# Spreading softmax reciprocals over the partitions: one transfer per tile over 128 partitions in place of halves of 64, with a new operation sequence

## The chip, the cores and the metric

One core of one Trainium2 chip runs the whole program. The time is device microseconds of that core, the median of several executions; most executions of one kernel here agree within 0.5%. Where a ratio is given, it is the mean time of one kernel's runs over the mean of the other's of the same rounds on the same chip, so it is not quite the ratio of the medians quoted beside it.

## The reference

Attention over 4 batches, 8 heads, 768 positions and 64 features, followed by a layer with a swish in the middle. Three heads (0, 2, 6) see every earlier key, the other five see 4 sink keys and a window of 64.

```python
scores = scale * np.matmul(q, k.transpose(0, 1, 3, 2))
scores = np.where(mask[None], scores, -1e9)
a = np.exp(scores - np.max(scores, axis=-1, keepdims=True))
a = a / (np.sum(a, axis=-1, keepdims=True) + 1e-09)      # the division that this case is about
x = np.matmul(a, v)  # -> [4 * 768, 8 * 64]
h = x @ w_in                                             # 512 -> 2048
out = (h / (1 + np.exp(-beta * h))) @ w_out              # 2048 -> 512
```

## The kernel before

The work is cut into 8 units of 384 positions (units 2b and 2b+1 are the halves of batch b). A unit's attention result lies in PSUM as four tiles of 128 partitions x 384 positions; a tile holds two heads, one on partitions 0 to 63 and one on 64 to 127. It must be multiplied by 1/sum, and 1/sum is one number per head and position, so it has to be copied to the 64 partitions of its head. From unit 2 on this is done with transfers: sums out of PSUM, gathered into a compact tile (`rec`), reciprocal, out to DRAM (`rd`), and back with every row read 64 times (`R`). That last step is "the spread".

```python
PAIRS/XT: x tile t holds the heads XT[t] = [(1, 0), (2, 3), (4, 5), (6, 7)][t]
ORDER = [[1, 0, 2, 3, 4, 5, 6, 7], [2, 6, 0, 3, 5, 7, 1, 4]]    # rows of rd, even and odd units

def sums_turn(x):                     # gather: 8 rows of 384 -> 96 partitions of 32
    for p, step, c, n in ([(0, 16, 0, 8)], [(96, 1, 3, 5), (0, 32, 0, 3)])[x.u]:
        sp.dma_start(out=x.rec[c * CR:(c + n) * CR, :],
                     in_=x.sc[p:p + (n - 1) * step + 1:step, :].rearrange("p (c n) -> p c n", n=32))

def spread_w(x):                      # reciprocals to DRAM
    sp.dma_start(out=x.rd.rearrange("h (c n) -> (h c) n", n=32), in_=x.rec)

def spread_r(x):                      # the spread: halves of 64 partitions
    for i in range(2):
        ...                           # which tiles one transfer can take
        for t in ts:
            sp.dma_start(out=x.R[i * D:(i + 1) * D, t, :],
                         in_=bass.AP(..., [[0, D], [(a[1] - a[0]) * NQ, len(a)], [1, NQ]]))

def norm(x, g):                       # tiles 0, 1 (g = 0) and 2, 3 (g = 1)
    dve.tensor_mul(x.xT[:, 2 * g:2 * g + 2, :], o[:, :, 0:NQ], x.R[:, 2 * g:2 * g + 2, :])

def mm1(x, fi):                       # first layer; needs all four tiles of xT
    for pi in range(NP):
        pe.matmul(h[:, 0:NQ], w_in_sb[...], x.xT[:, pi, :], start=(pi == 0), stop=(pi == NP - 1))
# ... everything else cut
```

Each engine is given its instructions in a fixed order. That order comes from a list, `SEQUENCE`, which was searched with estimated costs; so the list is part of the tuning, and the estimates for the spread (`dma=[4.1, 4.4]`) decide how much other work stands between the spread and its use. All stores, transposes and spreads, and all loads but four of k, are issued by SyncE, one after the other.

The softmax here doesn't subtract the row's maximum and nothing guards it: scores larger than these inputs give would overflow.

Of the kernel before, what the change touches and what calls it, by code (L numbers as in the profile page):

```python
# [20 lines left out]
NQ = 384  # L21
# [7 lines left out]
QUARTERS = [[[1, 0], [2, 3], [4, 5], [6, 7]], [[2], [6], [0], [3, 5, 7, 1, 4]]]  # L29
ROWS = [16, 1]  # L30

NE = [16, 24]
ORDER = [[1, 0, 2, 3, 4, 5, 6, 7], [2, 6, 0, 3, 5, 7, 1, 4]]
# [4 lines left out]
    474, 475, 0, 2, 468, 10, 8, 6, 4, 469, 473, 14, 466, 477, 463, 471, 12, 81, 1, 478, 77, 25, 3, 16, 26, 9,  # L38
    33, 11, 479, 20, 35, 34, 5, 27, 18, 36, 28, 7, 29, 42, 31, 30, 13, 53, 480, 32, 82, 15, 50, 41, 37, 51,
    464, 38, 54, 52, 44, 17, 45, 47, 39, 48, 85, 23, 46, 24, 79, 40, 49, 78, 56, 89, 21, 104, 55, 57, 490, 19,  # L40
    43, 58, 59, 22, 100, 60, 61, 101, 482, 62, 83, 476, 80, 91, 73, 63, 90, 485, 102, 74, 75, 484, 64, 103,
    76, 116, 465, 117, 65, 118, 66, 86, 67, 69, 119, 120, 491, 87, 68, 492, 122, 70, 71, 481, 123, 72, 483,
    121, 470, 125, 494, 520, 500, 84, 493, 126, 106, 524, 107, 105, 521, 93, 528, 525, 489, 532, 526, 486, 95,
    128, 127, 529, 112, 92, 88, 522, 97, 536, 530, 113, 495, 114, 537, 108, 115, 109, 124, 129, 538, 503, 540,
    501, 110, 541, 547, 111, 488, 542, 487, 548, 131, 134, 94, 132, 551, 505, 130, 135, 549, 137, 98, 138,
    139, 502, 555, 533, 133, 142, 140, 136, 504, 534, 559, 552, 141, 143, 510, 563, 96, 553, 556, 560, 144,
    99, 467, 561, 496, 155, 557, 499, 564, 145, 497, 157, 498, 156, 506, 515, 523, 146, 507, 570, 509, 527,
    565, 508, 571, 169, 147, 158, 531, 572, 161, 148, 149, 535, 511, 163, 150, 512, 151, 167, 153, 152, 574,
    513, 165, 514, 154, 578, 575, 159, 582, 173, 576, 579, 171, 586, 580, 583, 518, 218, 584, 517, 587, 516,
    588, 519, 592, 596, 593, 539, 597, 168, 543, 546, 170, 544, 550, 164, 598, 222, 188, 160, 554, 594, 189,  # L50
    162, 558, 166, 172, 184, 562, 185, 174, 186, 600, 187, 190, 193, 181, 191, 566, 196, 569, 192, 573, 175,
    194, 604, 220, 567, 198, 605, 219, 577, 601, 201, 221, 581, 199, 197, 585, 602, 225, 589, 200, 228, 608,
    590, 195, 606, 224, 203, 609, 612, 223, 204, 227, 610, 619, 202, 206, 613, 205, 623, 226, 620, 207, 614,
    176, 627, 621, 208, 177, 591, 628, 568, 631, 178, 624, 209, 629, 179, 210, 635, 625, 632, 545, 636, 633,
    229, 237, 637, 642, 239, 646, 238, 235, 650, 182, 643, 240, 647, 644, 595, 241, 211, 648, 654, 212, 242,
    472, 269, 599, 651, 249, 655, 652, 658, 236, 250, 656, 232, 603, 286, 252, 183, 607, 659, 254, 230, 660,
    213, 611, 257, 243, 251, 615, 255, 231, 180, 618, 622, 616, 273, 256, 626, 253, 244, 630, 245, 634, 247,
    246, 638, 258, 248, 641, 639, 645, 287, 233, 259, 617, 214, 260, 216, 215, 261, 649, 272, 653, 217, 271,
    280, 657, 234, 664, 276, 668, 288, 665, 661, 279, 669, 666, 275, 672, 662, 270, 676, 278, 670, 673, 262,
    680, 274, 677, 674, 684, 678, 277, 681, 691, 685, 682, 281, 695, 263, 686, 692, 699, 326, 283, 696, 693,  # L60
    703, 697, 700, 707, 704, 701, 714, 663, 705, 708, 718, 289, 715, 709, 722, 716, 290, 726, 264, 293, 667,
    719, 291, 671, 720, 675, 727, 329, 723, 730, 728, 315, 282, 724, 679, 731, 292, 328, 295, 732, 683, 284,
    298, 687, 296, 690, 294, 694, 319, 297, 300, 688, 698, 301, 285, 702, 303, 299, 265, 302, 304, 267, 327,
    689, 266, 305, 330, 268, 706, 306, 710, 307, 713, 711, 717, 370, 736, 317, 740, 721, 741, 321, 725, 737,
    318, 324, 729, 738, 322, 742, 733, 331, 316, 744, 325, 734, 748, 320, 745, 308, 752, 749, 746, 323, 756,
    750, 753, 763, 757, 754, 309, 767, 366, 758, 764, 771, 768, 765, 775, 769, 772, 779, 712, 773, 332, 786,
    780, 790, 776, 781, 334, 310, 777, 787, 739, 336, 788, 794, 335, 798, 791, 368, 377, 337, 795, 743, 369,
    339, 796, 747, 792, 338, 373, 802, 799, 346, 803, 800, 751, 349, 640, 804, 755, 333, 347, 350, 759, 367,
    762, 760, 341, 371, 766, 344, 340, 770, 374, 372, 342, 774, 345, 348, 351, 375, 778, 343, 354, 782, 376,
    352, 355, 313, 783, 353, 311, 378, 383, 356, 312, 785, 784, 357, 314, 789, 358, 793, 808, 812, 412, 816,  # L70
    813, 387, 817, 814, 797, 390, 386, 801, 388, 820, 818, 359, 392, 389, 821, 360, 805, 809, 416, 822, 395,
    824, 810, 391, 393, 828, 415, 806, 835, 829, 394, 839, 414, 836, 830, 397, 837, 361, 825, 843, 840, 826,
    847, 841, 844, 851, 845, 858, 396, 384, 811, 418, 815, 848, 379, 421, 398, 819, 849, 413, 859, 860, 852,
    862, 807, 853, 866, 863, 399, 870, 400, 419, 864, 867, 823, 871, 422, 874, 872, 364, 401, 417, 868, 875,
    362, 876, 420, 385, 402, 380, 363, 827, 735, 403, 365, 831, 404, 834, 832, 838, 423, 381, 842, 846, 429,
    880, 382, 833, 884, 881, 888, 885, 850, 886, 431, 882, 889, 854, 405, 432, 890, 857, 406, 861, 433, 426,
    865, 425, 855, 869, 424, 856, 430, 761, 873, 427, 434, 436, 892, 407, 877, 435, 896, 878, 893, 900, 897,
    894, 879, 907, 898, 901, 911, 908, 902, 915, 909, 912, 919, 916, 913, 923, 917, 920, 930, 924, 921, 934,
    925, 938, 935, 942, 931, 410, 932, 936, 408, 939, 883, 943, 409, 887, 411, 946, 891, 940, 443, 947, 952,
    446, 948, 895, 944, 444, 956, 953, 960, 954, 899, 445, 961, 447, 438, 962, 903, 439, 437, 906, 964, 441,  # L80
    440, 910, 904, 957, 448, 442, 905, 914, 428, 449, 918, 451, 922, 965, 452, 450, 926, 958, 453, 927, 966,
    929, 928, 454, 933, 455, 968, 972, 969, 979, 970, 937, 980, 983, 981, 941, 984, 945, 973, 985, 987, 974,
    456, 991, 988, 457, 995, 992, 989, 949, 993, 996, 955, 997, 1002, 950, 1006, 1003, 959, 1007, 1004, 458,
    1010, 1008, 1014, 1011, 1018, 1015, 1012, 963, 1016, 1019, 951, 967, 1020, 971, 975, 978, 976, 982, 977,
    986, 990, 994, 998, 1001, 999, 1005, 459, 461, 460, 1009, 462, 1013, 1017, 1021, 1024, 1022, 1028, 1025,
    1023, 1032, 1000, 1029, 1026, 1036, 1030, 1033, 1040, 1037, 1034, 1044, 1038, 1041, 1051, 1045, 1042,
    1055, 1046, 1052, 1059, 1056, 1053, 1063, 1057, 1060, 1067, 1064, 1061, 1073, 1065, 1068, 1076, 1027,
    1077, 1069, 1031, 1074, 1078, 1079, 1075, 1082, 1080, 1085, 1083, 1081, 1035, 1084, 1086, 1039, 1087,
    1043, 1047, 1050, 1048, 1054, 1049, 1058, 1062, 1066, 1070, 1088, 1071, 1089, 1072, 1092, 1090, 1091,
# [3 lines left out]
    "dggdaaadgddddaddaddagddaaagaaaggddggddaadaddddaggadaaddggddggaggadddadgaddaaadddaaadaadddddaadaaa"  # L93
# [95 lines left out]
def kernel(  # L189
# [557 lines left out]
    def sums_d(x):  # L747
# [4 lines left out]
        for g, heads in enumerate(QUARTERS[x.u]):  # L752
            ops = []
            for i, h in enumerate(heads):
                r = ROWS[x.u] * i
                if RETR[h]:
                    ops += [(one[:, 31 - r:63 - r], q0, n, e) for (kb, q0, n, e) in x.work[h]]
                else:
                    ops += [(one[:, 31 - r:63 - r], 0, NQ, x.work[h]), (one[:, 31 - r:63 - r], None, NE[x.u], x.edge[h])]
            assert ops[0][1:3] == (0, NQ)  # L760
            todo.append(ops)
# [17 lines left out]
    def sums_turn(x):  # L779

        x.rec = rp.tile([8 * CR, 32], F32, name="rec")
        for p, step, c, n in ([(0, 16, 0, 8)], [(96, 1, 3, 5), (0, 32, 0, 3)])[x.u]:
            sp.dma_start(out=x.rec[c * CR:(c + n) * CR, :],
                         in_=x.sc[p:p + (n - 1) * step + 1:step, :].rearrange("p (c n) -> p c n", n=32))
# [8 lines left out]
    def spread_r(x):  # L793
# [3 lines left out]
        for i in range(2):  # L797
            d = at[i][1] - at[i][0]
            ts = [slice(0, NP)] if all(at[i][t] == at[i][0] + t * d for t in range(NP)) else [slice(0, 3, 2), slice(1, 4, 2)]
            for t in ts:  # L800
                a = at[i][t]
# [160 lines left out]
    add = plan.add  # L962
# [278 lines left out]
```

## Time and profile before

| | before |
|---|---|
| median of 3 runs | 244.12 us (243.6 to 245.04) |
| span of the profiled run | 242.7 us |
| TensorE busy | 226.1 us, 93% |
| granted TensorE clock, mean | 0.993 |
| first issue of a spread to its last landing, six units | 6.4 to 8.6 us |

How to read the lines: PE is TensorE, PEld its weight loads, DVE VectorE, ACT ScalarE, POOL GpSimd, and SPq SyncE issuing transfers. `out<-in` names what is written and what is read: `wf`, `q2f`, `k2f` and `vf` are loads of q, k, v and the weights, `c` and `vb` their copies in 16 bits, `QK` the transposed queries and keys, `KP` a packed copy of keys, `sp` and `b` results in PSUM, `xT` the normalised tiles, `osb` an output block on its way to DRAM. The granted clock is the share of its full clock that TensorE was allowed. "The chain" starts at the last instruction and is followed back, at each step, to what released it. In the kernel before it consists of:

```profile
PE 50%; DMA 24%; SPq 12%; DVE 4%; POOL 4%; issue 2%; ACT 1%; ACTq 0%; POOLq 0%; DVEq 0%
```

Half of the chain is TensorE at work, and most of the rest lies in the first 145 us, where loads, and SyncE's issuing of them, are the last thing that something waited for. The grouped waits (who waited for whom: total, times, longest):

```profile
POOL c L112 <- DMA wf<-in_q_dram: 15.7, 4, 13.5
...
POOL KP L112 <- DMA QK<-c: 13.7, 3, 6.0
POOL vb L112 <- DMA wf<-in_v_dram: 13.6, 7, 5.7
...
ACT osb L112 <- DMA out_dram<-osb: 4.1, 2, 2.1
...
PE sp L112 <- DMA QK<-c: 1.8, 2, 1.0
...
PE b L112 <- DVE xT L112: 1.3, 2, 1.1
```

GpSimd waiting for loads costs nothing as long as TensorE does not wait for GpSimd, and it hardly does: the largest group of such waits, weight loads that wait for a weight's 16-bit copy, adds up to 2.1 us.

### The profile page before, as it was taken

The page shows a single profiled execution, that of the slowest core. Times are in us where ns is not written, and L with a number is a line of the kernel's source. Part 1 is how long each engine was busy: PE and PEld are TensorE (multiplying, and loading weights), DVE is VectorE, ACT ScalarE, POOL GpSimd, SP SyncE. Part 2 cuts the span into 40 slices and gives each one's busy share as a digit, 9 for nine tenths or more (in the row PEclk, how much of TensorE's full clock was granted, in tenths as well). Part 3 has the DMA queues.
Part 4 walks back from the last instruction along what each step waited for, and adds up shares of the span by engine and source line. Part 5 has one row for each costly group of instructions (what it writes and reads, how often), then busy time and mean ns, then how long its engine had stood idle before and what let it go on. Part 6 is the DMA issues. An engine that isn't in the chain of part 4 may idle for free.

```text
span 242.7 us, 6088 instructions
## 1 busy us (share of the span) xinstructions
PE 226.1 (93%) x2388; PEld 127.7 (53%) x2388; DVE 158.8 (65%) x359; ACT 137.9 (57%) x231; POOL 87.5 (36%) x201
## 2 busy tenths in 40 slices
PE   7795889899979989899999989999999999999994
PEld 6562456455544445446554545564465455455553
DVE  4895789864786759479575457787566847336620
ACT  3657686266859607562489548745674745208611
POOL 6204757595791937354717300624200000000000
PEclk9999799999999999999999999999999999999999
DMA  6999699999979997999999999999720110802012
GB/s 208 272 321 333 199 252 349 290 289 198 190 199 178 217 172 167 194 244 198 237 179 246 205 167 178 212 175 240 203 61 3 43 45 7 221 3 86 0 43 86
DMA packets 92108, 43.14 MB, mean 178 GB/s; under 512 B 75936, under 2 KB 84848, under 8 KB 92080
## 3 DMA queue, kind: packets, MB, share of 16 engines
q1 hardware_dynamic: 90992, 41.98, 75.8%
q10 hardware_dynamic: 1088, 0.79, 1.0%
q8 instruction: 18, 0.29, 0.5%
q14 instruction: 10, 0.08, 0.1%
HBM read 32.38 MB, written 6.37 MB: 160 GB/s over the span
## 4 chain that ended last, share of the span: by engine, by line
PE 50%; DMA 24%; SPq 12%; DVE 4%; POOL 4%; issue 2%; ACT 1%; ACTq 0%; POOLq 0%; DVEq 0%
PE b L112 46%; SPq L112 12%; DMA wf<-in_moe_w_in_dram 9%; PE sp L112 4%; DMA wf<-in_v_dram 3%; DMA R<-rd 3%; DMA vf<-in_v_dram 3%; DMA wf<-in_k_dram 2%; DMA k2f<-in_k_dram 2%; DVE gT L112 2%; DMA QK<-c 2%; POOL w_in L112 2%; POOL c L112 2%; ACT t L112 1%; DVE xT L112 1%
## 5 line engine op out<-in xcount | busy, mean ns | idle before, releaser
L112 ACT ACTIVATE t<-b,beta_h 128x384 f32<-128x384 f32 x128 | 72.4, 583 | 47.9 <-PE b L112 36.1
L112 DVE SCALAR_TENSOR_TENSOR gT<-t,b 128x384 bf16<-128x384 f32 x128 | 68.8, 551 | 40.4 <-ACT t L112 36.8
L112 PE MATMUL b<-xT,w_in 128*128 128x384 bf16 x512 | 92.8, 330 | 2.0 <-POOL w_in L112 1.3
L112 PE MATMUL b<-w_out,gT 128*128 128x512 bf16 (+1 forms) x400 | 91.7, 371 | 0.0
L112 PEld LDWEIGHTS <-w_in 128*128 128x128 bf16 x512 | 49.4, 99 | 39.6 <-issue 3.9
L112 PEld LDWEIGHTS <-gT 128*128 128x128 bf16 x400 | 37.0, 98 | 38.5 <-issue 2.2
L112 ACT ACTIVATE es<-sp 128x768 bf16<-128x768 f32 (+2 forms) x64 | 48.6, 806 | 12.7 <-PE sp L112 12.5
L112 POOL CAST c<-wf 128x256 bf16<-128x256 f32 x60 | 22.5, 422 | 26.3 <-DMA wf<-in_q_dram 15.7
L112 PE MATMUL sp<-QK 64*64 64x64 bf16 (+6 forms) x402 | 18.8, 233 | 4.8 <-DMA QK<-c 1.8
L112 ACT ACTIVATE osb<-b 128x512 f32<-128x512 f32 (+1 forms) x13 | 7.4, 566 | 23.0 <-PE b L112 18.9
L112 PEld LDWEIGHTS <-QK 64*64 64x64 bf16 (+1 forms) x402 | 10.1, 105 | 15.5 <-issue 12.1
L112 POOL CAST vb<-wf 128x512 bf16<-128x512 f32 x18 | 12.1, 689 | 15.5 <-DMA wf<-in_v_dram 13.6
L112 DVE TENSOR_TENSOR es<-es,mask_c 128x256 bf16<-128x256 bf16 (+2 forms) x32 | 14.4, 457 | 4.1 <-ACT es L112 3.9
L112 POOL COPY KP<-QK 128x64 bf16<-128x64 bf16 (+5 forms) x38 | 10.6, 328 | 16.3 <-DMA QK<-c 13.7
L112 DVE TENSOR_TENSOR xT<-sp,R 128x768 bf16<-128x768 f32 (+3 forms) x18 | 11.6, 684 | 7.3 <-PE sp L112 5.8
L112 POOL CAST w_in<-wf 128x512 bf16<-128x512 f32 x16 | 9.8, 654 | 14.9 <-DMA wf<-in_moe_w_in_dram 14.9
L112 DVE TENSOR_TENSOR es<-es,mask_s 128x800 bf16<-128x800 bf16 (+5 forms) x24 | 13.4, 570 | 2.3 <-ACT es L112 2.2
L112 PE MATMUL sp<-es,vb 128*64 128x64 bf16 (+3 forms) x243 | 13.7, 237 | 0.0
L112 DVE COPY vs<-vb 64x1536 bf16<-64x1536 bf16 (+4 forms) x19 | 10.2, 550 | 2.9 <-POOL vb L112 2.7
L112 PEld LDWEIGHTS <-vb 128*64 128x64 bf16 x243 | 11.6, 111 | 0.4
L112 POOL CAST w_out<-wf 128x512 bf16<-128x512 f32 x16 | 10.1, 678 | 2.3 <-DMA wf<-in_moe_w_out_dram 2.2
L112 POOL COPY vs<-vb 64x1536 bf16<-64x1536 bf16 (+2 forms) x7 | 9.2, 1318 | 4.3 <-issue 4.1
(91 smaller groups left out, 167.5 us busy)
## 6 DMA issues: line engine op xcount, KB each, us to landing
out_dram<-osb SPq DMA_DIRECT2D x23, 256.0 KB
wf<-in_v_dram SPq DMA_DIRECT2D x18, 256.0 KB
wf<-in_moe_w_out_dram SPq DMA_DIRECT2D x4, 1024.0 KB
wf<-in_q_dram SPq DMA_DIRECT2D x15, 256.0 KB
wf<-in_k_dram SPq DMA_DIRECT2D x15, 256.0 KB
R<-rd SPq DMA_DIRECT2D x9, 384.0 KB
wf<-in_moe_w_in_dram SPq DMA_DIRECT2D x4, 768.0 KB
q2f<-in_q_dram SPq DMA_DIRECT2D x12, 192.0 KB
```

The lines of the kernel that those rows point to most:

```text
L112: ins = f(*a, **k)
```

## The change

The intent: one transfer per tile fills all 128 partitions; each tile is ready on its own, so the first two can be normalised early; odd units, whose heads lie irregularly, need no special cuts. The row order for odd units is changed so that a tile's second head always stands behind its first. The estimates for the spread are raised, and the sequence is searched again with them.

```diff
-ORDER = [[1, 0, 2, 3, 4, 5, 6, 7], [2, 6, 0, 3, 5, 7, 1, 4]]
+ORDER = [[1, 0, 2, 3, 4, 5, 6, 7], [2, 6, 1, 4, 3, 5, 7, 0]]
 ...                                                  # the rows of the sums follow this order
-        for i in range(2):
-            ...
-                sp.dma_start(out=x.R[i * D:(i + 1) * D, t, :],
-                             in_=bass.AP(..., [[0, D], [(a[1] - a[0]) * NQ, len(a)], [1, NQ]]))
+        for t in range(NP):
+            sp.dma_start(out=x.R[:, t, :], in_=bass.AP(src.tensor, src.offset + at[0][t] * NQ,
+                                                       [[(at[1][t] - at[0][t]) * NQ, 2], [0, D], [1, NQ]]))
 ...
-            add("sp", [1.33, 2.65][u], lambda: spread_r(x), ..., dma=[4.1, 4.4][u],
+            add("sp", [1.4, 1.8][u], lambda: spread_r(x), ..., dma=[6.2, 6.0][u],
 ...                                                  # SEQUENCE and CHOICE: new throughout, cut
```

## The prediction

> **What bounds the kernel now.** I read the page first, then the chain of waits in order of time, then the waits grouped by who waited for whom, then SyncE's own timeline of DMA issues, and last the trace's records of single packets and semaphore updates.
>
> ```profile
> span 242.7 us, 6088 instructions
> PE 226.1 (93%) x2388; PEld 127.7 (53%) x2388; DVE 158.8 (65%) x359; ACT 137.9 (57%) x231; POOL 87.5 (36%) x201
> ...
> PE   7795889899979989899999989999999999999994
> ...
> DMA  6999699999979997999999999999720110802012
> ```
>
> TensorE is busy 93% of the span. Of the 16.6 us it is not, most lies before 50 us; from 145 us on it is never idle in any length. So there is at most some 7% to win, and whatever makes TensorE wait in the second half adds to the time one for one. The DMA row is near full up to slice 28 (about 170 us): loads run at the edge there.
>
> ```profile
> 76.21 0.33 SPq L112
> ...
> 80.23 0.70 SPq L112
> 80.93 0.04 issue
> 80.97 7.90 DMA R<-rd
> 88.87 0.04 DVEq L112
> 88.91 0.04 issue
> 88.95 1.83 DVE xT L112 x2
> 90.78 0.04 issue
> 90.83 7.65 PE b L112 x45
> ```
>
> This is the chain of waits around the first of six spreads (units 2 to 7 of the work, one each). The reciprocals go to DRAM (76.21), come back copied over 64 partitions for each head (80.23, landed 88.87), VectorE normalises with them, and TensorE's next layer starts. So one spread is already on the path.
>
> ```profile
> DVE xT L112 <- DMA R<-rd: 1.3, 1, 1.3
> ```
>
> The grouped waits say how tightly: once, 1.3 us. At the other five, the last spread transfer lands before the normalisation starts by 1.9, 2.8, 1.7, 4.0 and 4.1 us (landing times from the semaphore updates; starts 112.20, 139.23, 161.44, 182.00, 215.40).
>
> ```profile
> 171.39 1.34 SPq L112 DMA_DIRECT2D R<-rd  x2
> ...
> 204.66 1.97 SPq L112 DMA_DIRECT2D R<-rd  x3
> 206.67 0.59 SPq L112 DMA_DIRECT2D q2f<-rd  x1
> ```
>
> Those two spreads have the queue nearly alone: the first lands whole at 178.0, the second at 211.3, both 6.6 us after the first issue. Of this 1.5 us pass before the first packet moves, 4.2 to 4.4 us are packets, the rest is the landing.
>
> **What the Trainium skill says.** (1) "DMA: Bandwidth & Descriptors", section "Rules for kernel authors", advises against two transfers to disjoint partition halves and for one over 128 partitions: the intent of the change. (2) The same page, section "Why a DMA increments its semaphore by 16 and not by 1", says that a transfer runs on k engines, k being the largest number up to 16 that divides the size of the slowest dimension (not of size 1) of both sides. The rules table repeats it: a small outermost dimension of size c confines the transfer to c engines. The trace of the kernel before agrees exactly. The transfers that gather the sums have source outer sizes of 8, 5 and 3 against 96, 60 and 36 partitions, and their semaphores get 8, 5 and 3 updates from engines, plus one from the sequencer; the 64-partition halves get 16. (3) Its "Specifications" give about 27 GiB/s per engine. The trace: 1,536-byte packets take 62 to 65 ns at best (24 GB/s), 6,144-byte ones 234 ns (26 GB/s). (4) "TensorE: Matmul & The Clock Gate", part 1 on the clock gate, says that an idle window of some 3.4 us halves the clock. The windows view shows a granted clock of 0.83 between 20 and 30 us, where TensorE had several gaps.
>
> **The change part by part.**
>
> Removed: the halves, two transfers per even unit (64 partitions x 4 tiles x 1,536 bytes) and three per odd one. Added: four per unit, each 128 partitions x 1,536 bytes. In the built program the source of each is [2, 64, 384] with a step of 0 in the middle, the destination [128, 1, 384]. This is the same mismatch as in the gathering of the sums. The rule gives k = 2, one engine for each half of the partitions. Bytes and packets stay the same: 512 packets of 1,536 bytes. Before, an engine had 32 of them; now two engines have 4 x 64 = 256 each, and fourteen have none. 256 x 65 ns = 16.6 us where 4.2 us stood. With the same 1.5 us ahead and 0.9 us behind, a spread lands 19.1 us after its first issue instead of 6.6: 12.5 us later (estimate from the measured packet).
>
> SyncE's issues: 0.60 to 0.70 us each for the 64-partition form, 0.33 to 0.44 us for plain 128-partition ones, but 0.74 to 0.9 us where the dimensions mismatch. So four cost 1.4 to 3.2 us instead of 1.3 (even) or 2.5 (odd): small beside the rest.
>
> A gain: the first two tiles now wait for two transfers only, so their normalisation (about 0.9 us of VectorE) can be done before the last transfer lands. I take 0.9 us off at each unit.
>
> Moved: the sequence. I counted the matmuls in program order between a unit's sums and the first matmul that needs its spread, at measured rates (0.166 us per first-layer matmul, 0.217 per second-layer one, the small ones scaled). Units 2 to 7, before: 19.3, 27.1, 28.5, 24.8, 23.1, 25.0 us. After: 21.2, 29.0, 29.4, 24.7, 25.1, 26.8. That is 1.9, 1.9, 0.9, -0.1, 2.0 and 1.8 us more room. On SyncE, six small loads of v rows left the stretch ahead of unit 2's spread (1.71 + 1.50 us on the timeline), and six were put ahead of the spreads of units 4 and 6 (about 2.4 us each). The changed plan counts on 6.2 us of transfer where it had 4.1, so it made room for about 2 us, not for 12.5.
>
> Stall before the normalised tiles are ready = 12.5 - slack - added room + shift on SyncE - 0.9:
> unit 2: 12.5 - 0.1 - 1.9 - 3.2 - 0.9 = 6.4;
> unit 3: 12.5 - 1.9 - 1.9 - 0.9 = 7.8;
> unit 4: 12.5 - 2.8 - 0.9 + 2.4 - 0.9 = 10.3;
> unit 5: 12.5 - 1.7 + 0.1 - 0.9 = 10.0;
> unit 6: 12.5 - 4.0 - 2.0 + 2.4 - 0.9 = 8.0;
> unit 7: 12.5 - 4.1 - 1.8 - 0.9 = 5.7.
>
> Do the stalls add up? On VectorE the next unit's reciprocal stands after this unit's normalisation in program order from unit 3 on, so a late normalisation delays the next spread too; a stall gives the next unit no lead. Only the time from the end of a normalisation to the next reciprocal can shrink: it was 5.2, 6.0 and 4.4 us for units 4, 5 and 6, where the sums stand ahead of the stall on TensorE. I take 4, 4 and 3 us off. Sum: 6.4 + 7.8 + 6.3 + 6.0 + 5.0 + 5.7 = 37.2 us. Stalls longer than 3.4 us let the clock drop: about 0.8 us each, six times, 4.8 us (estimate). 244.1 + 37.2 + 4.8 = 286 us.
>
> **The rivals.**
>
> First rival: the transfers spread over 16 engines after all, because the partition side decides. Then each is a plain 128-partition transfer, the spread costs some 4 to 6 us, the first half is normalised sooner, the new sequence's 2 us of room holds, and SyncE saves up to 0.8 us on odd units. For it: the plan's own figures (6.2 us, 0.35 us per issue) look like such a transfer. Against it: the three counts of 8, 5 and 3. Time: 240 to 246 us.
>
> Second rival: k is 2, but the load side pays most. SyncE's ring to two engines fills; the loads behind the spread stand in the same rings and land up to 13 us late. Up to 170 us the DMA row is near full, so each of units 2 to 5 would lengthen the load pipeline by up to 13 us, and loads of q, k and v become the wait that ends last. For it: on the chain of waits loads stand at 112, 129 and 140 us, and an issue of three loads after the first spread already took 6.71 us. Against it: TensorE's stalls give the loads time to catch up, so most of this is the same time counted twice. Time: 290 to 310 us.
>
> Third rival: the spread is longer but hidden, because TensorE has second-layer matmuls to do meanwhile. The room found above is 20 to 29 us from sums to need, but 16 to 24 us of it are used up to the landing in the kernel before. Only if the new order put the spread's issue several microseconds earlier would this hold, and I see that for unit 2 alone. Time: 250 to 265 us.
>
> **Range and chances.** The two-engine reading rests on three counts of the same form in this trace, so I give 0.8 to clearly slower; within it the times run from 255 to 308 us, by how far loads and stalls overlap. 0.15 goes to the first rival ending within 2%, and 0.05 to its ending over 2% faster, since TensorE's 226.1 us of work does not shrink and only the early gaps could. Point: 286 us; range 252 to 306 us.
>
> **What would show each step.** Right: each spread transfer's semaphore gets two updates from engines; 1,536-byte packets span about 17 us per unit, two at a time; the wait of VectorE's normalisation for the spread grows from 1.3 us to tens of microseconds in six places; TensorE's busy time stays near 226 us at about 80% of the span; the DMA row falls to low digits where two engines work alone. The size would be wrong if the loads dominate: then casts on GpSimd, not the normalisation, show the long waits. The prediction as a whole is wrong if the spread transfers get 16 updates each and land in about 7 us.

## The result, and the profile after

The changed kernel takes 297.86 us (297.18 to 298.49, 3 runs) against 244.12: ratio 1.219, 95% interval 1.212 to 1.227. The page of the changed kernel (parts 1 and 2, where each digit is a fortieth of the span in tenths, and the summary of the chain):

```profile
span 296.8 us, 6069 instructions
PE 238.9 (80%) x2359; PEld 133.1 (45%) x2385; DVE 153.5 (52%) x354; ACT 141.6 (48%) x238; POOL 89.4 (30%) x199
...
PE   8689789999994499908999169974994699995995
...
PEclk9857999999999599986999859996899599999999
DMA  7998899997912696149961999197713002131001
...
PE 34%; DMA 31%; SPq 23%; DVE 4%; ACT 4%; issue 2%; DVEq 0%; ACTq 0%
```

TensorE is now idle for 296.8 - 238.9 = 57.9 us where it was 16.6. The holes are visible as low digits in its row, six groups of them, from slice 13 on. The DMA row has holes at about the same places: low digits (1, 2, 1) where two of sixteen engines work alone. The clock row dips at or just after five of the six holes (slices 14, 18 to 19, 23 to 24, 28 to 29 and 32), and once before any of them (slices 2 to 4). In three of the six units (2, 6 and 7) the chain of waits goes through the landing of the spread; in the other three it goes through SyncE's queue, the issues of the spread and those behind it. In unit 2:

```profile
79.40 0.56 SPq L112
...
80.00 0.91 SPq L112
...
80.96 1.65 SPq L112
...
82.66 16.45 DMA R<-rd
...
99.23 0.97 DVE xT L112
```

These answer to the lines around 80 us in the prediction: the last spread transfer took 7.90 us there and takes 16.45 here, from its issue (3.66 us, within the 16.45) to its landing, after three issues of growing length. The grouped waits (the first line answers to the one in the prediction, the others to those shown before):

```profile
DVE xT L112 <- DMA R<-rd: 46.5, 12, 7.6
...
ACT osb L112 <- DMA out_dram<-osb: 37.5, 3, 18.0
...
POOL KP L112 <- DMA QK<-c: 32.2, 4, 16.4
PE b L112 <- DVE xT L112: 24.5, 7, 8.0
...
PE sp L112 <- DMA QK<-c: 11.0, 4, 9.5
```

The normalisation waited 1.3 us for the spread, and waits 46.5 us now. But the waits for the transposed keys (`QK<-c`) and for the output stores grew too, and one of TensorE's own largest stops, 9.5 us, is for a transpose, not for the spread. GpSimd's waits for loads of q, k and v grew as well (for q from 15.7 to 23.4 us). The prediction had named a sign to tell its theory from its second rival, which of the two waits grows, and both grew. So the profile alone leaves two suspects.

The trace's semaphore records count the engines. Each spread transfer gets three updates: two when its packets are done and one early one, 0.4 to 0.5 us after SyncE has finished the issue, long before the landing; the prediction puts the early one down to the sequencer. Of the kernel before, each got 16. The 1,536-byte packets take 65 to 71 ns in the median, 512 per unit (98 to 121 ns in the even units of the kernel before, where sixteen engines worked at once), but they span 17.3 to 18.5 us, and a spread has landed whole 19.2 to 20.3 us after its first issue.

### The profile page after: what moved, and what is told of

Read it like the earlier page. It is cut to its first block, busy times and chain, and to the rows that moved or that the text cites. A ratio compares the mean times of both kernels' runs of the same rounds, so it can differ in the third digit from the quotient of the medians.

```text
span 296.8 us, 6069 instructions
## 1 busy us (share of the span) xinstructions
PE 238.9 (80%) x2359; PEld 133.1 (45%) x2385; DVE 153.5 (52%) x354; ACT 141.6 (48%) x238; POOL 89.4 (30%) x199
## 4 chain that ended last, share of the span: by engine, by line
PE 34%; DMA 31%; SPq 23%; DVE 4%; ACT 4%; issue 2%; DVEq 0%; ACTq 0%
PE b L112 30%; SPq L112 23%; DMA R<-rd 17%; DMA q2f<-in_q_dram 6%; PE sp L112 5%; DMA rd<-rec 3%; DMA QK<-c 2%; DMA wf<-in_v_dram 1%; ACT es L112 1%; DMA out_dram<-osb 1%; DMA k2f<-in_k_dram 1%; ACT t L112 1%; DVE gT L112 1%; DVE es L112 1%; DVE xT L112 1%
## 5 line engine op out<-in xcount | busy, mean ns | idle before, releaser
L112 PE MATMUL b<-xT,w_in 128*128 128x384 bf16 x512 | 98.1, 342 | 26.7 <-DVE xT L112 23.5
L112 PEld LDWEIGHTS <-w_in 128*128 128x128 bf16 x512 | 51.1, 102 | 61.6 <-issue 29.4
L112 ACT ACTIVATE es<-sp 128x768 bf16<-128x768 f32 (+3 forms) x64 | 49.0, 806 | 21.3 <-PE sp L112 21.0
L112 DVE TENSOR_TENSOR xT<-sp,R 128x768 bf16<-128x768 f32 (+3 forms) x18 | 12.4, 692 | 50.1 <-DMA R<-rd 46.5
L112 PE MATMUL sp<-QK 64*64 64x64 bf16 (+6 forms) x402 | 21.4, 254 | 19.8 <-DMA QK<-c 11.0
L112 POOL CAST c<-wf 128x256 bf16<-128x256 f32 x60 | 23.1, 431 | 42.6 <-DMA wf<-in_q_dram 23.4
L112 PEld LDWEIGHTS <-QK 64*64 64x64 bf16 (+1 forms) x402 | 11.2, 113 | 25.7 <-issue 13.7
L112 POOL COPY KP<-QK 128x64 bf16<-128x64 bf16 (+4 forms) x36 | 9.9, 326 | 32.2 <-DMA QK<-c 32.2
L112 DVE TENSOR_TENSOR es<-es,mask_c 128x256 bf16<-128x256 bf16 (+2 forms) x32 | 12.9, 418 | 4.9 <-ACT es L112 4.7
L112 POOL CAST w_in<-wf 128x512 bf16<-128x512 f32 x16 | 9.9, 648 | 16.6 <-DMA wf<-in_moe_w_in_dram 16.6
L112 DVE TENSOR_SCALAR osb<-b 128x512 f32<-128x512 f32 x11 | 7.6, 688 | 12.7 <-PE b L112 6.7
L112 POOL COPY vs<-vb 64x1536 bf16<-64x1536 bf16 (+2 forms) x9 | 12.2, 1361 | 3.2 <-issue 2.8
L112 DVE TENSOR_TENSOR es<-es,mask_s 128x800 bf16<-128x800 bf16 (+5 forms) x24 | 12.1, 516 | 2.1 <-ACT es L112 1.9
```

Of the source, the lines that this page charges most:

```text
L112: ins = f(*a, **k)
```

## The experiments

Eleven runs, each on the same chip as runs of the kernel before (medians 243.48 to 244.01 us there). Every result was correct except where said.

**1. Which part of the change costs: the transfers or the sequence?** Two runs separate them. The first keeps the new sequence and the new row order and goes back to halves of 64:

```diff
-        for t in range(NP):
-            sp.dma_start(out=x.R[:, t, :], in_=bass.AP(..., [[(at[1][t] - at[0][t]) * NQ, 2], [0, D], [1, NQ]]))
+        for i in range(2):
+            ts = ([slice(0, NP)] if not x.u else [slice(0, 3, 2), slice(1, 4, 2)] if i == 0 else [slice(0, 1), slice(1, 4)])
+            for t in ts:
+                sp.dma_start(out=x.R[i * D:(i + 1) * D, t, :], in_=bass.AP(..., [[0, D], [step, len(a)], [1, NQ]]))
```

> The changed kernel's sequence and head order, with the spread in 64-partition halves again (two transfers per even unit, four plus the small one per odd unit). Theory 'two engines': the halves get 16 engine updates each, a spread lands some 6.6 us after its first issue, the sequence alone costs or gains little: 240 to 250 us. Rival 'the new sequence is what is slow': stays above 280 us.

Measured: 240.09 us, ratio 0.985 (0.980 to 0.990). The spread lands 6.7 to 8.1 us after its first issue, with 16 updates. The second takes the new transfers with the old sequence:

```diff
-SEQUENCE, CHOICE = the changed kernel's
+SEQUENCE, CHOICE = those of the kernel before
```

> The new transfers with the sequence and engine choice of the kernel before. Theory 'two engines': two engine updates each, landing 19 to 20 us after the first issue, and without the 2 us of room that the new sequence made: 290 to 310 us. Rival 'the new sequence is what is slow': 244 to 250 us.

Measured: 305.37 us, ratio 1.252. So the transfers are the whole loss, and the new sequence is a gain under both: 305.4 to 297.9 us with the new transfers (ratios 1.252 and 1.219), 243.5 to 240.1 with the halves. In the profile of the new sequence with halves the chain is TensorE nearly throughout:

```profile
PE 85%; DVE 4%; DMA 4%; ACT 4%; issue 2%; SPq 0%
```

Such shares are not to be leaned on: the same kernel profiled again (experiment 5) shows PE 66% and DMA 15% at nearly the same time.

**2. Is it the number of engines, or another property of the new form?** Four runs change nothing but how the source's 64 repeats are written. Each tile's transfer is cut into its two halves; then the 64 repeats are written as 64, as 8 x 8, as 4 x 16 and as 2 x 32. Bytes, packets, transfers and instructions are the same in all four; only the outermost size differs.

```diff
-            sp.dma_start(out=x.R[:, t, :], in_=bass.AP(..., [[(at[1][t] - at[0][t]) * NQ, 2], [0, D], [1, NQ]]))
+            for i in range(2):
+                sp.dma_start(out=x.R[i * D:(i + 1) * D, t, :],
+                             in_=bass.AP(..., [[0, D], [1, NQ]]))                 # 16
+                             in_=bass.AP(..., [[0, k], [0, D // k], [1, NQ]]))    # k = 8, 4, 2
```

> The changed kernel with each tile's transfer cut into its two halves of 64 partitions (eight transfers of 64 x 1,536 bytes; one transfer group per tile is kept, so what waits for which tile is kept). Theory 'two engines': 16 engine updates each, packets of a unit within 4 to 5 us, 240 to 252 us, with some 5 us of SyncE issues per unit as its price. Rival 'waiting tile by tile, or many transfers, is what is slow': above 280 us.

> As the tile halves, the source's 64 repeats written as 8 x 8: eight engines each. Theory 'two engines' (a spread takes 512 packets x 65 ns divided by the engines used, but not less than the 5 us in which SyncE issues eight transfers): eight engine updates, a landing 7 to 9 us after the first issue, 242 to 247 us. Rival 'any number under 16 is served worse': near the 254.6 us of four engines.

> As the tile halves, but the source's 64 repeats written as 4 x 16, so that by the rule four engines serve each transfer: same bytes, packets and transfers. Theory 'two engines': four engine updates, 128 packets x 65 ns = 8.3 us of packets per unit, a landing some 4 us later than with 16 engines, of which the sequence's room hides about half: 248 to 265 us. Rival 'the form of the issue, not the engine count': same time as the tile halves with 16.

> As the tile halves, the 64 repeats written as 2 x 32: two engines each, with the partitions still in halves of 64. Theory 'two engines': two engine updates, a landing 19 to 20 us after the first issue, 290 to 305 us, as the changed kernel's 298 us. Rival 'the 128-partition form has a cost of its own beside the engine count': clearly under 285 us.

| outermost size of the source | updates per transfer | 512 x 65 ns / engines | span of the packets | landed after first issue | time |
|---|---|---|---|---|---|
| 64 | 16 | 2.1 us | 5.5 to 6.8 us | 7.1 to 8.4 us | 243.57 us |
| 8 | 8 + 1 | 4.2 us | 5.9 to 6.7 us | 7.9 to 8.7 us | 243.98 us |
| 4 | 4 + 1 | 8.3 us | 9.2 to 10.2 us | 11.3 to 13.0 us | 254.57 us |
| 2 | 2 + 1 | 16.6 us | 17.4 to 18.1 us | 19.8 to 20.3 us | 299.11 us |
| 2, over 128 partitions (the change) | 2 + 1 | 16.6 us | 17.3 to 18.5 us | 19.2 to 20.3 us | 297.86 us |

(One of the 48 transfers of the first row shows 14 updates in the records, the others 16.) The landing follows packets divided by engines, down to where the eight issues themselves take some 5 us. The time follows the landing, with a threshold: 8 engines cost nothing, 4 cost 11 us, 2 cost 55 us. The 128-partition form has no cost of its own: with two engines the halves are as slow. In the run with four engines the normalisation begins to wait, and the output stores much more so:

```profile
ACT osb L112 <- DMA out_dram<-osb: 25.0, 4, 9.5
...
DVE xT L112 <- DMA R<-rd: 3.9, 5, 1.5
```

In its counterpart with 16 the normalisation does not wait for the spread at all, and the wait for the stores is 2.6 us. At four engines already, what stands behind the spread is late.

**3. What is it that is late: the reciprocals, or what is issued behind them?** The theory was that the normalisation waits and that the loads' lateness is the same time counted twice. First test: take the wait away by taking its reason away. The normalisation multiplies with a constant column, so that nothing reads the spread, while the two-engine transfers go on filling the queue. Its output is wrong, which doesn't matter for the time.

```diff
-            dve.tensor_mul(x.xT[:, 2 * g:2 * g + 2, :], o[:, :, 0:NQ], x.R[:, 2 * g:2 * g + 2, :])
+            dve.tensor_mul(x.xT[:, 2 * g:2 * g + 2, :], o[:, :, 0:NQ], beta_h[:, 0:1].unsqueeze(2).to_broadcast([128, 2, NQ]))
 ...                            # the other four products likewise
```

> The changed kernel with its two-engine spreads, but the normalisation multiplies with a constant column in place of the spread reciprocals (a wrong result on purpose): nothing waits for the spreads any more, they only occupy the queue. Theory 'the late reciprocals themselves are most of the loss': 248 to 270 us. Rival 'the loads and transposes issued behind the spread are what is late': stays at 280 us or more. If everything is the wait of the normalisation: 240 to 246 us.

Measured: 287.5 us, ratio 1.179. Only 10 us of the 54 come back. This is the rival's result: loads and transposes behind the spread hold the kernel up even when nobody waits for the spread. The grouped waits of this run say where:

```profile
ACT osb L112 <- DMA out_dram<-osb: 42.5, 3, 17.8
...
PE b L112 <- ACT osb L112: 17.4, 2, 9.5
PE sp L112 <- DMA QK<-c: 16.8, 3, 8.9
```

ScalarE waits for the buffer of an output block whose store has not landed (42.5 us), and TensorE waits for ScalarE (17.4 us). TensorE also waits for transposed keys (16.8 us). That these stores and transposes are late because they are stuck behind a spread is seen in SyncE's timeline of the changed kernel (start, duration, what was issued):

```profile
79.40 6.92 SPq L112 DMA_DIRECT2D R<-rd  x4
86.36 12.54 SPq L112 DMA_DIRECT2D wf<-in_k_dram  x3
...
151.09 7.20 SPq L112 DMA_DIRECT2D R<-rd  x4
158.41 13.05 SPq L112 DMA_TRANSPOSE QK<-c  x3
...
173.79 1.48 SPq L112 DMA_DIRECT2D rec<-sc  x2
```

The tile halves with 16 engines, and then the kernel before, in the first of these stretches:

```profile
76.19 5.88 SPq L112 DMA_DIRECT2D R<-rd  x8
82.18 2.21 SPq L112 DMA_DIRECT2D wf<-in_k_dram  x3
```

```profile
80.23 1.35 SPq L112 DMA_DIRECT2D R<-rd  x2
81.68 6.71 SPq L112 DMA_DIRECT2D wf<-in_k_dram  x3
```

Three loads of keys take 12.5 us to issue behind a spread on two engines, and 2.2 or 6.7 us behind one on sixteen, by how long the spread's own issues took. From the first issue of the spread to the last of the loads it is 8.2 us in both runs with sixteen engines and 19.5 us with two, about as long as the spread takes to land (19.7 us). A reading that fits, though no run tested it by itself: a transfer that uses all sixteen engines cannot be issued while two of them have no room for more.

A control was needed, because the constant operand could have had a cost of its own: the same edit with the tile halves on 16 engines.

> The control of the run without the normalisation's wait (287.5 us with two-engine spreads): the same constant in the normalisation, but the spreads as tile halves on 16 engines. Theory 'what is left at 287.5 us is the queue behind two-engine transfers': 240 to 245 us. Rival 'the constant operand or the freed order costs time of its own': above 260 us.

Measured: 244.16 us, ratio 1.002 (result wrong). So the constant costs nothing, and what is left at 287.5 us comes from the two-engine transfers in the queue.

Second test, the reverse: reciprocals late, queue free. The spreads are tile halves on 16 engines, and VectorE repeats each normalisation, with the same result, until it ends about where the two-engine spread would have let it end.

```diff
+        for _ in range(1 + ([(1, 9), (1, 5), (1, 9), (1, 5), (1, 9), (0, 3)][x.n - 2][g])):
             if not (g and moved(x, 6)):
                 dve.tensor_mul(x.xT[:, 2 * g:2 * g + 2, :], o[:, :, 0:NQ], x.R[:, 2 * g:2 * g + 2, :])
 ...
```

> The tile halves on 16 engines (243.6 us), but VectorE repeats each normalisation (same result) so often that it ends about where the two-engine spread would let it end: 1 extra pass on the first half and 9 on the second in even units, 1 and 5 in units 3 and 5, 0 and 3 in unit 7, some 51 us of VectorE in all. The queue is left alone. Theory 'late reciprocals by themselves cost nearly the whole loss, and so do the late loads: one cause that holds the kernel up in two ways at once': 278 to 295 us. Rival 'the loads behind the spread are the loss, the late reciprocals only fill the same time': under 262 us.

Measured: 296.35 us, ratio 1.212, just over the expected range. The second halves of the normalisation end at 98.0, 131.3, 168.0, 199.2, 229.6 and 269.3 us, against 100.2, 133.4, 171.3, 204.0, 232.3 and 273.1 in the changed kernel, so the imitation is close. The spreads land after 7.2 to 9.5 us. The grouped waits show TensorE waiting for the normalisation:

```profile
PE b L112 <- DVE xT L112: 26.6, 8, 8.9
...
PE sp L112 <- DVE xT L112: 17.0, 2, 8.9
```

Together the four runs and the changed kernel make a table of two causes:

| | queue free (16 engines) | queue with two-engine spreads |
|---|---|---|
| normalisation on time | 243.6 us (tile halves), 244.2 us (constant) | 287.5 us (constant) |
| normalisation late | 296.4 us (repeated passes) | 297.9 us (the change) |

Either cause alone costs 43 to 53 us, both together 54. They run at the same time, behind the same slow transfers, so neither can be read off by removing it alone. One caution: the imitation keeps VectorE busy where the changed kernel keeps it waiting. In unit 2 of the changed kernel VectorE ran nothing between its two halves of the normalisation (91.66 to 99.23 us), so it does nothing else in either case there; but this is an imitation and not the same program.

**4. Does the fallen clock cost on top?** In the changed kernel the granted clock fell to 0.914 from 0.993, and the same work keeps TensorE busy 12.8 us longer. Not all of the fall comes from the stops: in the windows view the clock is 0.77 in the first 30 us, before any spread (0.94 in the kernel before), and 0.91 from 90 us on (1.00). The test puts 98 idle matmuls of 512 columns into the stops of units 2, 3, 5 and 7:

```diff
+        for _ in range({2: 34, 3: 28, 5: 22, 7: 14}.get(x.n, 0) if fi == 0 else 0):
+            pe.matmul(h, ident, w_out_sb[0][:, 0, :], start=True, stop=True)
```

> The changed kernel with 34, 28, 22 and 14 idle matmuls of 512 columns (0.216 us each) ahead of the first layer of units 2, 3, 5 and 7, where TensorE stands still for the spread; the result is unchanged. Theory 'the granted clock falls in the stalls and that costs on top of them': granted clock from 0.91 to 0.94 or more, 289 to 295 us. Rival 'only the stalls count': 297 us or more.

Measured: 297.95 us, ratio 1.223 against 1.219; granted clock 0.948.

```profile
PE 255.1 (86%) x2483; PEld 139.6 (47%) x2483; DVE 155.2 (52%) x354; ACT 141.9 (48%) x238; POOL 88.8 (30%) x199
```

Of the 255.1 us some 98 x 0.216 = 21.2 us are the idle matmuls, so the real work took about 234 us, 5 us less than in the changed kernel (an estimate); the time did not move. Each of the four groups of idle matmuls had ended before the normalisation did, so they held nothing up. The windows from 90 us on show that the clock rose in the stops too (0.94 against 0.91), and not only at the start (0.89 against 0.77). For that part the theory that the clock costs on top falls; the rest of the lost clock was not given back, and whether it costs was not tested. The normalisations of units 2 and 3 end 33.2 us apart in the changed kernel and 33.5 us apart here, though the clock no longer falls between them: what TensorE gains is lost again in the next stop.

**5. The best version, again.** The lead of the halves with the new sequence is only 1.5%, so it was timed once more with five rounds.

> The best version so far, timed again: halves of 64 on 16 engines with the new sequence. If its lead is real, 239 to 242 us and an interval wholly below 0.995 of the kernel before; if it was the chip, 243 to 245 us.

Measured: 241.03 us, ratio 0.987 (0.982 to 0.992). It beats both kernels. The interval is clear of 1 in both runs. Which of the sequence's many moves brings it was not tried. In its profile no wait of the normalisation for the spread is left.

## Why the prediction was right or wrong

The time lies inside the range (297.86 in 252 to 306), 12 us above the point of 286. The mechanism, two engines per transfer, was right; that the sum came so near was in part luck. By its own steps:

- **Two engines per transfer.** Right, and shown: two engine updates plus the early one, and the series over 16, 8, 4 and 2 engines gives 243.6, 244.0, 254.6 and 299.1 us with all else equal.
- **A landing 19.1 us after the first issue, 12.5 us later than before.** Right: 19.2 to 20.3 us, with packets of 65 to 71 ns in the median, as estimated.
- **Issues of 1.4 to 3.2 us per spread, "small beside the rest".** Wrong in size and in weight: four issues took 6.1 to 8.3 us, the third and fourth being the long ones (1.65 and 3.66 us in unit 2), and what stands behind them is held up with them.
- **The first half is normalised before the last transfer lands.** It was, in all six units; the trace shows the two halves of the normalisation apart, with up to 7.6 us of waiting between them.
- **The per-unit stops.** The normalisation of units 2 to 7 ends 9.4, 18.9, 30.3, 40.2, 48.4 and 55.3 us later than in the kernel before. These 55.3 us have two parts. From a unit's own reciprocal to the end of its normalisation it takes 10.1, 8.3, 8.3, 7.5, 9.3 and 6.8 us longer than before, 50.3 us in all. The prediction had 6.4, 7.8, 10.3, 10.0, 8.0 and 5.7, or 48.2 before its deduction: near in sum, but up to 3.7 us off in single units. In unit 2 it counted 3.2 us for six small loads that moved out of the way; the spread was issued only 0.8 us earlier (79.40 against 80.23).
- **"I take 4, 4 and 3 us off."** This is the step that failed most. The gap from the end of a normalisation to the next unit's reciprocal should have shrunk by that much in units 4 to 6. It went from 5.2, 6.0 and 4.4 us to 8.4, 8.4 and 3.4. The gathering of the next unit's sums is issued by SyncE too, behind loads and transposes that the spread holds up: in units 4 and 5 the sums are ready at 123.9 and 162.5 us and their gathering is issued at 136.95 and 173.79, 13.1 and 11.3 us later, where the kernel before took 1.9 and 2.6 us. Ready sums wait for a queue. The term of -11 us measured about +4.5 there and +5.0 over all units, which is the second part of the 55.3.
- **The clock, 4.8 us.** For the 0.8 us per stop the prediction shows no working. TensorE's busy time, expected near 226 us, came to 238.9, so the fall was larger than estimated; but the part of it that was given back by filling the stops left the time at 298 us. No cost on top of the stops was found.
- **The second rival, dismissed as "mostly the same time counted twice".** Half right. It is mostly the same time, since both causes together cost 54 us and not 96. But the first cause was not the only one to be counted: without any wait for the reciprocals, 287.5 us remain. The prediction named one mechanism as the cause where the kernel has two, each of which brings 43 to 53 of the 54 us by itself. The rival's own range, 290 to 310 us, holds the measured time better than the point of 286.
- **The first rival (16 engines after all).** False for this form; the run with halves shows that its time, 240 us, would have been right if it had been so.
- **The third rival (longer but hidden, 250 to 265 us).** False: with two engines the normalisation waits 46.5 us.

So the sum of 42.0 us met a measured 55.3 (end of the last normalisation, profiled runs; what follows it is 1.2 us shorter than before): the stalls were 2.1 us larger than counted, the gaps 16.0 us (+5.0 in place of -11), and the 4.8 us for the clock belong to no separate cost. Two errors of opposite sign, the lead that did not come and the clock, partly cancelled; that is the luck in it.

## What to carry to other kernels

Before merging transfers, read the outermost size of both sides: a broadcast source whose outer loop is 2 turns a 128-partition transfer into a two-engine one, and the count of semaphore updates in a trace tells it at once. A transfer that was confined to two engines did harm in two ways here: what it brought was late, and what was issued behind it on the same queue was late too; with one removed, the other still held the kernel up. And where a transfer set the stops, neither a higher clock nor idle work in the stop changed the time.

## What the Trainium skill lacked or had wrong

- "DMA: Bandwidth & Descriptors", section "Rules for kernel authors", advises one 128-partition transfer in place of two disjoint halves without the exception. Here the halves run on 16 engines and the single transfer on 2: 240.1 us against 297.9 with the same sequence. The exception follows from the same table's row on using all engines, which the runs confirm.
- The same page, section "Why a DMA increments its semaphore by 16 and not by 1", is right for this form (8, 4 and 2 engine updates for outer sizes of 8, 4 and 2, also where the source is DRAM and the step is 0). It does not say that few engines need not hurt: 8 engines took 243.98 us against 243.57 with 16, as the packets divided among 8 engines come to 4.2 us (65 ns each in the median) and the eight issues themselves take about 5 us.
- I found on none of the pages that I read how long a queue with a confined transfer holds up the issues behind it. Measured: 12.5 us for three loads that took 2.2 and 6.7 us behind spreads on 16 engines, and 0.56, 0.91, 1.65 and 3.66 us for the four spread issues in a row (unit 2).
- "TensorE: Matmul & The Clock Gate", part 1: the fall of the clock with stops agrees (0.91 from 90 us on, where the stops are, against 1.00 in the kernel before). That it costs time did not show where transfers set the pace: 0.94 there with filled stops, at the same 298 us.
